# Random-feature attention and a two-branch FFN on one core: where weights are fetched and in which order work is issued

## Chip, core and metric

The kernel runs on one core of a Trainium2 chip. TensorE (PE) does matrix products into PSUM; VectorE (DVE), ScalarE (ACT) and GpSimd (POOL) do element-wise work; SyncE (SP) issues most DMAs. ACT can issue DMAs too, from the same instruction stream that holds its activations. Each engine works through its own instructions in order, and waits on semaphores between engines. The metric is device time in microseconds (us), lower is better.

## What is computed

8 batches, 8 heads, 576 tokens, head size 64, 128 random features. The attention is linear: features of q and k, a sum over the tokens of a batch, a quotient. Its output, as 4608 rows of 512, goes through an FFN with no nonlinearity but a product of two branches.

```python
def phi(x):
    proj = np.einsum('bhsd,md->bhsm', x, omega)
    h = proj - np.sum(x * x, axis=-1, keepdims=True) / 2.0
    h = h - np.max(h, axis=-1, keepdims=True)
    return np.exp(h) / np.sqrt(m)
kv = np.einsum('bhsm,bhsd->bhmd', k_p, v); z = np.sum(k_p, axis=2)
num = np.einsum('bhsm,bhmd->bhsd', q_p, kv)
den = np.einsum('bhsm,bhm->bhs', q_p, z)[..., None] + 1e-06
a = x @ w1; b = x @ w2            # x: 4608 x 512; w1, w2: 512 x 1024
return (a * b @ w3) @ w_out       # w3: 1024 x 1024; w_out: 1024 x 512
```

The four weights arrive as float64. Everything else is float32.

## The kernel before

**Chunks.** The 4608 tokens are 36 chunks of 128. For chunk c of k: load (`kraw`), project on omega (`kpj`, 8 heads by 128 features), take the negated maximum (`nm`, L306), exponential (`ek`), and cut the result into two f16 halves, high and low (`in_parts`, L330 and L141 or L143). Each of the 8 batches covers 4 to 6 chunks; `kv_batch` multiplies their features with v (`kvp`, L411) into `kv`. For chunk c of q: the same up to `eq`, then a DMA transpose (`eqT`), a product with `kv` (`nu`, L440), the quotient (`xs`, L455), two f16 halves (`xhl`, L477) and another DMA transpose into `xT`. f32 numbers are multiplied as three f16 products of halves (`PASSES`). The first chunks are projected directly in f32 instead (`whole`: k below `KF`, q below `QF`, L287); the later ones need a norm, a scale and a split first (`khl`, `qhl`, L152 and L155, then L294). v is scaled or split likewise (`vhl`).

**FFN.** `gate` multiplies `xT` with w1 and w2 (`ab`, L678), then the two results with each other (`asb`, L688). `project_out` multiplies that with W, the product of w3 and w_out (`o`, L707).

**Weights.** They come in 20 units of 1 MB through `from_float64`: `fetch` (a DMA on ACT's queue, L526) into one of three raw slots of the `arena`, `magnitude` (Abs on ACT, L534) and `bits` (four DVE passes, L540 to L545). A slot is free again after the last pass. W's blocks then form on PE: `W_block` makes 8 of them, each from one unit of w3 and four blocks of w_out (`wp`, L618). The first four are first addends, copied from PSUM into `Wb` by ACT (L630). The last four are second addends: here the first addend is brought into the same PSUM bank by a product with an identity matrix (L616), and ACT copies the sum back. `w12_load` also sums magnitudes of w1 and w2 on PE (`l`, L570); `w12_split` and `W_split` cut the weights into f16 halves.

**What sets the order.** `ORDER` lists the weight units (o: w_out, W: a block, 1 and 2: w1 and w2, a, b, S: splits); `SKEW` spreads their steps over ticks, `PER` says how many ticks of weights go into each slot of a plan. `put(slot, rank, fn)` places the steps of each chunk; `LAGS`, `KOFF`, `QOFF`, `KVD`, `KV_LAG` and others shift them. From this program order a scheduler makes each engine's instruction order, by priority, which follows program order unless `tc.high_priority(offset=n)` moves a step up (n below zero: down). PSUM has two banks-of-two for `kpj`, `qpj`, `nu` and `kvp` (`banks`), and four single banks for the rest.

## Time and profile before

| | us |
|---|---|
| runs before | 844.92, 848.72, 849.43 (median 848.72) |
| the profiled execution, its own time | 844.82 |
| its span, first to last instruction | 843.0 |
| PE busy | 786.0 |
| DVE busy | 577.0 |
| ACT busy | 437.6 |
| POOL busy | 228.5 |
| mean granted clock of PE | 0.977 |

The span is 1.8 us below the execution's own time. Busy times of engines overlap, so their sum says nothing; what counts is which engine is waited for at each place. Lines such as "L618 PE MATMUL wp<-w12b" name the source line, the engine, and the program's names of the tile written and the tiles read. A bracket behind a row gives the idle time of that engine just before it and the instruction whose end ended that idle time.

### The profile page before, as it was taken

Reading aid. Unit: us, or ns where it says so; the run is one execution under the profiler, and the core shown is the slowest. Engines: PE = TensorE matmul, PEld = TensorE weight load, DVE = VectorE, ACT = ScalarE, POOL = GpSimd, SP = SyncE. Lnnn points to the kernel's source line nnn. Section 1 sums busy time; section 2 is a strip of 40 time slices with the busy share of each in tenths; the row PEclk is TensorE's granted clock in tenths of the full one; section 3 lists DMA queues with packets and bytes.
Section 4 is the critical chain, followed back from the end, with each engine's and each line's share of the span. In section 5 each row is a group of like instructions: output and inputs, shape, how many; then the busy total and the mean of one; then the engine's idle time right before and its main releaser. Section 6 shows DMA issues by size and latency. Waiting matters only on the chain.

```text
span 843.0 us, 19911 instructions
## 1 busy us (share of the span) xinstructions
PE 786.0 (93%) x8353; PEld 580.1 (69%) x8353; DVE 577.0 (68%) x1049; ACT 437.6 (52%) x793; POOL 228.5 (27%) x210
## 2 busy tenths in 40 slices
PE   1968799799979999999999999999999999999998
PEld 1436455696858777777777777777777777777773
DVE  5695967886888788768777877787778765452000
ACT  2674746884655557656555565466545433232221
POOL 0000001221435324533333334333433332221110
PEclk8889699999989999999999999999999999999999
DMA  8584659334435454535343634354333342321000
GB/s 302 187 267 145 200 151 213 89 64 72 114 93 115 73 153 89 101 76 126 91 87 81 137 85 87 79 126 101 78 84 67 65 85 66 76 51 38 26 14 37
DMA packets 142521, 88.38 MB, mean 105 GB/s; under 512 B 116704, under 2 KB 116832, under 8 KB 142432
## 3 DMA queue, kind: packets, MB, share of 16 engines
q1 hardware_dynamic: 134944, 66.15, 35.8%
q10 hardware_dynamic: 7488, 20.97, 7.6%
q8 instruction: 65, 1.06, 0.5%
q14 instruction: 24, 0.20, 0.1%
HBM read 49.35 MB, written 9.44 MB: 70 GB/s over the span
## 4 chain that ended last, share of the span: by engine, by line
PE 46%; DVE 16%; ACT 9%; issue 7%; DMA 1%; POOL 1%; SPq 0%; DVEq 0%; ACTq 0%; POOLq 0%
PE ab L678 24%; PE o L707 15%; DVE nm L306 3%; PE kvp L411 3%; DVE khl L155 2%; DVE ke L320 2%; PE nu L440 2%; DVE qe L320 2%; ACT ek L143 2%; ACT qe L321 1%; PE qpj L294 1%; DVE xs L455 1%; DMA kraw<-kT 1%; DVE asb L688 1%; ACT xhl L476 1%
## 5 line engine op out<-in xcount | busy, mean ns | idle before, releaser
L678 PE MATMUL ab<-xT,w12b 128*128 128x256 f16 (+1 forms) x3840 | 390.7, 262 | 5.7 <-DMA xT<-xhl 4.7
L678 PEld LDWEIGHTS <-w12b 128*128 128x128 f16 x3840 | 340.1, 98 | 43.5 <-issue 4.9
L707 PE MATMUL o<-Wb,arena 128*128 128x512 f16 x864 | 195.7, 383 | 1.0 <-DVE p2p L195 1.0
L693 POOL TENSOR_TENSOR arena<-asb,arena 128x512 f16<-128x512 f32 x72 | 92.8, 1288 | 316.0 <-ACT arena L692 316.0
L707 PEld LDWEIGHTS <-arena 128*128 128x128 f16 x864 | 82.3, 98 | 98.1 <-issue 4.2
L688 DVE TENSOR_TENSOR asb<-ab,asb 128x512 f32<-128x512 f32 x72 | 49.5, 687 | 115.9 <-PE ab L678 91.8
L330 POOL TENSOR_TENSOR eq<-qe,eq 128x1024 f16<-128x1024 f32 x34 | 74.5, 2192 | 135.0 <-DVE eq L141 80.6
L618 PE MATMUL wp<-w12b 128*128 128x512 f32 x128 | 64.6, 656 | 12.5 <-DVE w12b L545 12.4
L330 POOL TENSOR_TENSOR ek<-ke,ek 128x1024 f16<-128x1024 f32 x26 | 56.6, 2179 | 70.9 <-ACT ek L143 62.5
L692 ACT CAST arena<-asb 128x512 f16<-128x512 f32 x72 | 44.1, 612 | 58.0 <-DVE asb L688 57.9
L155 DVE SCALAR_TENSOR_TENSOR qhl<-qraw,s,qhl 128x512 f16<-128x512 f32 x31 | 51.4, 1657 | 18.1 <-ACT qhl L152 18.1
L687 ACT ACTIVATE asb<-ab 128x512 f32<-128x512 f32 x72 | 42.3, 587 | 34.7 <-PE ab L678 30.9
L321 ACT ACTIVATE qe<-qe,ln_e,es 128x1024 f32<-128x1024 f32 x31 | 38.4, 1238 | 41.2 <-DVE qe L320 41.1
L321 ACT ACTIVATE ke<-ke,ln_e,es 128x1024 f32<-128x1024 f32 x26 | 32.2, 1238 | 51.1 <-DVE ke L320 51.1
L476 ACT ACTIVATE xhl<-xs,p2r 128x512 f16<-128x512 f32 x36 | 26.0, 721 | 62.1 <-DVE p2r L198 60.3
L618 PEld LDWEIGHTS wp<-w12b 128*128 128x128 f32 x128 | 26.2, 210 | 45.7 <-issue 30.7
L306 DVE TENSOR_REDUCE nm<-kpj 128x8 f32<-128x1024 f32 x36 | 43.8, 1217 | 9.8 <-PE kpj L287 5.1
L711 ACT ACTIVATE o<-o,oscs 128x512 f32<-128x512 f32 x36 | 24.3, 675 | 40.8 <-PE o L707 33.6
L411 PE MATMUL kvp<-vhl,ek 128*128 128x65 f16 (+1 forms) x880 | 41.8, 208 | 3.4 <-DVE xs L455 3.4
L306 DVE TENSOR_REDUCE nm<-qpj 128x8 f32<-128x1024 f32 x36 | 43.7, 1215 | 0.2
L440 PE MATMUL nu<-kv,eqT 128*128 128x65 f16 (+1 forms) x960 | 34.1, 195 | 8.4 <-DMA eqT<-eq 7.6
L141 DVE CAST eq<-qe 128x1024 f16<-128x1024 f32 x31 | 21.5, 692 | 29.0 <-ACT qe L321 29.0
(121 smaller groups left out, 929.2 us busy)
## 6 DMA issues: line engine op xcount, KB each, us to landing
kraw<-kT SPq DMA_DIRECT2D x36, 256.0 KB, 2.8
qraw<-qT SPq DMA_DIRECT2D x36, 256.0 KB, 2.7
vraw<-v SPq DMA_DIRECT2D x36, 256.0 KB, 4.3
out<-o SPq DMA_DIRECT2D x36, 256.0 KB, 2.3
arena<-w3T ACTq DMA_DIRECT2D x8, 1024.0 KB, 6.5
arena<-w ACTq DMA_DIRECT2D x8, 1024.0 KB, 6.2
arena<-wo ACTq DMA_DIRECT2D x4, 1024.0 KB, 5.1
eqT<-eq SPq DMA_TRANSPOSE x72, 3.1
```

Source lines behind the costliest of these rows:

```text
L155: nc.vector.scalar_tensor_tensor(lo, src, s, hi, ALU.mult, ALU.subtract)
L306: nc.vector.tensor_reduce(nm, pj, AX.X, ALU.max, negate=True)
L321: nc.scalar.activation(e, e, AF.Exp, scale=es, bias=ln_e)
L330: (nc.vector if lo == "d" else nc.gpsimd).tensor_tensor(t[:, 1], e, t[:, 0], ALU.subtract)
L411: nc.tensor.matmul(ps[:, h // 4, h % 4], x, y, start=n == 0, stop=n == len(mm) - 1)
L440: nc.tensor.matmul(nu[r0:r1, h // 4, h % 4], t[:, x, place(h), r0:r1], kvs[b][:, y, h], start=n == 0, stop=n == 2,)
L618: nc.tensor.matmul(ps, w[:, j, k * P : (k + 1) * P], guest[:, j], start=j == j0, stop=j == HALF - 1,)
L678: nc.tensor.matmul(ps[:, k], w12[m][i][cc][:, a, r * P : (r + 1) * P], x[:, b, cc, off : off + T], start=j == 0, stop=j == len(mm) - 1,)
L688: nc.vector.tensor_tensor(asb, ab[1], asb, ALU.mult)
L692: nc.scalar.copy(h[:, 0], asb)
L693: nc.gpsimd.tensor_tensor(h[:, 1], asb, h[:, 0], ALU.subtract)
L707: nc.tensor.matmul(ps, hs[c, f][0][:, a], W[f][:, b], start=i == 0, stop=i == len(mm) - 1)
```

## The change

The fetches of weights go to SyncE's queue, but for the sixth (`FQ`). The first unit of w_out is fetched and converted in two halves (`cuts=2`), and k's first two loads go to ACT's queue right behind the first two fetches. omega gets a tile of its own and two queues, its split stands first (`OM_AT`), and a small Abs comes ahead of everything on ACT (`T0`). W's second addend is added by VectorE straight from PSUM. Steps get priorities (`PR`): splits of q, k and v 200, x's turn 100, v's scale 20, conversions of weights -20. `V_ACT` moves the scaling of the first v chunks to ACT, `KF`, `QF` project three more chunks in f32, `EH` to `DQ` move casts and exponentials of some chunks, and the tables of the plan change, `KV_LAG` from 6 to 4 among them, by which a batch's `kvp` from the fifth on stands ahead of two gate products and a q projection and right behind a k projection.

```diff
-QF = 5
-KF = 10
+QF = 6
+KF = 12
 VF = 9
-V_ACT = 0
+V_ACT = 1
+PR = {'vscale': 20, 'split': 200, 'vsplit': 200, 'x': 100, 'bits': -20}
+START = 1
+WADD = 1
+FQ = 'sssssas'
+T0 = 1
+OM1 = 1
...
-ORDER = 'ooW1W1aW2W2booWWWW11a22bS'
+ORDER = 'ooW1W1aW2W2oboWWWW11a22bS'
...
-KV_LAG = 6
+KV_LAG = 4
-OM_AT = 4
-K_BEHIND = 1
+OM_AT = 0
+K_BEHIND = 0
...
+    def ahead(kind):
+        return tc.high_priority(offset=PR[kind]) if PR.get(kind) else nullcontext()
+
+    def early(kind, fn):
+        def go(*args):
+            with ahead(kind):
+                return fn(*args)
+
+        return go
...
+        nc.scalar.dma_start(om_raw[0:D], omT)
+        nc.sync.dma_start(om_raw[D:P], omT)
...
+    if T0:
+        nc.scalar.activation(om_sq, ln_e, AF.Abs)
...
-            nc.scalar.dma_start(raw.rearrange("p (j i) -> p j i", j=src.shape[1]), src)
+            for k in range(0, src.shape[1], step):
+                {'a': nc.scalar, 's': nc.sync, 'p': nc.gpsimd}[pick(FQ, nfetch[0])].dma_start(raw[:, k : k + step], src[:, k : k + step])
...
-    for u in units[:RAW64_BUFS]:
+    for n, u in enumerate(units[:RAW64_BUFS]):
         u[0]()
         u[0] = None
+        if START and n < 2:
+            load(kT, n, "k", nc.scalar)
...
-                if j0:
+                if j0 and not WADD:
                     nc.tensor.matmul(ps, ident, Wb[:, i + k + 1], start=True, stop=False)
...
-                nc.scalar.copy(Wi, ps)
+                if j0 and WADD:
+                    nc.vector.tensor_tensor(Wi, ps, Wi, ALU.add)
+                else:
+                    nc.scalar.copy(Wi, ps)
...
-            put(at0 - NOFF[2], 8, splits)
+            put(at0 - NOFF[2], 8, early("split", splits))
```

How it moves instructions, at three places. First the fetches. On ACT before, the stretch behind the first block's product; a DMA row is a fetch of 1 MB (`w3T`, `w2`), the rows around it are copies of W, square sums of v, Abs and exponentials:

```order
L630 COPY Wb_82<-wp_0_0_137 128x512
L169 ACTIVATE junk_v0_2_225,vam_0_186<-vraw_2_180 128x512
L630 COPY Wb_82<-wp_0_1_142 128x512
L526 DMA arena_98<-w3T 128x4x512
L169 ACTIVATE junk_v0_3_244,vam_0_186<-vraw_3_182 128x512
L566 ACTIVATE wab_0_2_0_271<-w12b_96 128x1024
L169 ACTIVATE junk_v0_4_269,vam_0_186<-vraw_4_184 64x512
L534 ACTIVATE arena_98<-arena_98 128x1024
L318 ACTIVATE ek_2_246<-kpj_2_247,nm_258 128x128 x8
L526 DMA arena_98<-w2 128x2x1024
```

On SyncE after, the same units, with loads of k, v and q between them:

```order
L568 DMA arena_100<-w1 128x2x1024
L257 DMA kraw_2_171<-kT 128x512
L387 DMA vraw_0_184<-v 128x512
L387 DMA vraw_1_186<-v 128x512
L568 DMA arena_100<-w3T 128x4x512
L387 DMA vraw_2_188<-v 128x512
L387 DMA vraw_3_190<-v 128x512
L387 DMA vraw_4_192<-v 128x512
L257 DMA kraw_3_218<-kT 128x512
L257 DMA kraw_4_264<-kT 128x512
L257 DMA qraw_0_346<-qT 128x512
L568 DMA arena_100<-w3T 128x4x512
```

A fetch stood behind ACT's own work on data; now it stands behind other loads and their slots alone.

Second, VectorE around the first `xhl`. Before, from the 13th conversion's last pass (the w12b row that reads the arena) to `xs` of chunk 0:

```order
L449 TENSOR_SCALAR gd_593<-nu_0_568 128x8
L545 SCALAR_TENSOR_TENSOR w12b_96<-arena_98 128x1024
L453 RECIPROCAL gr_595<-gd_593 128x8
L155 SCALAR_TENSOR_TENSOR w12b_96<-w12b_96,ws_544 128x512
L455 TENSOR_TENSOR xs_0_597<-nu_0_568,gr_595 128x512
```

and on to `xhl` of chunk 0:

```order
L306 TENSOR_REDUCE nm_632<-qpj_1_621 128x8
L462 TENSOR_REDUCE mx_599<-xs_0_597 128x1
L316 TENSOR_SCALAR nm_632<-nm_632 128x8
L468 TENSOR_SCALAR mx_599<-mx_599 128x1
L195 TENSOR_SCALAR p2p1_4_610<-mx_599 128x1
L198 RECIPROCAL p2r1_4_612<-p2p1_4_610 128x1
L473 TENSOR_SCALAR pt_0_614<-p2p1_4_610,pv_285 128x1
L155 SCALAR_TENSOR_TENSOR w12b_96<-w12b_96,ws_544 128x512
L306 TENSOR_REDUCE nm_662<-kpj_6_651 128x8
L477 SCALAR_TENSOR_TENSOR xhl_0_616<-xs_0_597,p2r1_4_612,xhl_0_616 128x512
```

After, from the same pass to the same `xs`:

```order
L592 SCALAR_TENSOR_TENSOR w12b_98<-arena_100 128x1024
L586 TENSOR_SCALAR arena_100<-arena_100 128x1024
L175 SCALAR_TENSOR_TENSOR w12b_98<-w12b_98,ws_560 128x512
L589 SCALAR_TENSOR_TENSOR arena_100<-arena_100 128x1024
L175 SCALAR_TENSOR_TENSOR w12b_98<-w12b_98,ws_560 128x512
L592 SCALAR_TENSOR_TENSOR w12b_98<-arena_100 128x1024
L175 SCALAR_TENSOR_TENSOR w12b_98<-w12b_98,ws_560 128x512
L485 TENSOR_SCALAR gd_601<-nu_0_576 128x8
L584 TENSOR_SCALAR arena_100<-arena_100 128x1024
L489 RECIPROCAL gr_603<-gd_601 128x8
L175 SCALAR_TENSOR_TENSOR w12b_98<-w12b_98,ws_560 128x512
L491 TENSOR_TENSOR xs_0_605<-nu_0_576,gr_603 128x512
```

and on from the row behind its two reductions and a small row to `xhl` of chunk 0:

```order
L586 TENSOR_SCALAR arena_100<-arena_100 128x1024
L504 TENSOR_SCALAR mx_607<-mx_607 128x1
L342 TENSOR_REDUCE nm_670<-kpj_6_659 128x8
L215 TENSOR_SCALAR p2p1_4_618<-mx_607 128x1
L589 SCALAR_TENSOR_TENSOR arena_100<-arena_100 128x1024
L218 RECIPROCAL p2r1_4_620<-p2p1_4_618 128x1
L509 TENSOR_SCALAR pt_0_622<-p2p1_4_618,pv_293 128x1
L161 CAST eq_1_652<-qe_1_642 128x1024
L352 TENSOR_SCALAR nm_670<-nm_670 128x8
L683 TENSOR_TENSOR Wb_82<-wp_4_0_683,Wb_82 128x512
L513 SCALAR_TENSOR_TENSOR xhl_0_624<-xs_0_605,p2r1_4_620,xhl_0_624 128x512
```

Passes of the 14th and 15th conversion, a cast of `eq_1` and the first add into `Wb` now stand between; the pass itself stands earlier against the other work.

Third, VectorE between the gate product of chunk 4's first unit and the scale of q 8 and k 13 (`norm_q8_k13`), by which their splits go. Before:

```order
L688 TENSOR_TENSOR asb_4_0_2549<-ab_4_0_1_2524,asb_4_0_2549 128x512
L306 TENSOR_REDUCE nm_2579<-qpj_7_2554 128x8
L320 TENSOR_TENSOR qe_7_2581<-qpj_7_2554,nm_2579 128x1024
L306 TENSOR_REDUCE nm_2616<-kpj_12_2591 128x8
L320 TENSOR_TENSOR ke_12_2618<-kpj_12_2591,nm_2616 128x1024
L141 CAST eq_7_2584<-qe_7_2581 128x1024
L141 CAST ek_12_2590<-ke_12_2618 128x1024
L688 TENSOR_TENSOR asb_4_1_2678<-ab_4_1_1_2653,asb_4_1_2678 128x512
L184 TENSOR_SCALAR norm_q8_k13_2687<-norm_q8_k13_2687 128x3
```

After:

```order
L342 TENSOR_REDUCE nm_2442<-kpj_12_2417 128x8
L356 TENSOR_TENSOR ke_12_2444<-kpj_12_2417,nm_2442 128x1024
L161 CAST ek_12_2416<-ke_12_2444 128x1024
L743 TENSOR_TENSOR asb_4_0_2504<-ab_4_0_1_2479,asb_4_0_2504 128x512
L342 TENSOR_REDUCE nm_2534<-qpj_7_2509 128x8
L352 TENSOR_SCALAR nm_2534<-nm_2534,es_2365 128x8
L161 CAST eq_7_2546<-qe_7_2536 128x1024
L743 TENSOR_TENSOR asb_4_1_2607<-ab_4_1_1_2582,asb_4_1_2607 128x512
L485 TENSOR_SCALAR gd_2637<-nu_6_2612 128x8
L204 TENSOR_SCALAR norm_q8_k13_2649<-norm_q8_k13_2649 128x3
```

k chunk 12's reduction, add and cast have moved ahead of that gate product; q chunk 7 has a small row in place of its 128x1024 add.

More of the change, by code (lines that the diff above doesn't have):

```diff
@@ L224, in tile_favor_attention_then_bilinear_ffn, with load @@
     raws, scales = {}, {}
-    def load(src, c, name):
+    def load(src, c, name, queue=nc.sync):
         t = at.tile([P, NP, P], F32, tag=f"{name}raw", name=f"{name}raw_{c}", bufs=RAW_BUFS)
-        nc.sync.dma_start(t, src[c])
+        dma = queue.dma_start(t, src[c])
         raws[name, c] = t
+        if name == "q" and c < 2 and QD >= 0:
+            tc.add_manual_dep(
+                dma.ins,
+                converted[QD].name,
+                mybir.DependencyInfo(mybir.DependencyClass.Sync, mybir.DependencyReason.DATA),
+                reason="q_load",
+            )
     sums = []
@@ L599, in wo_load @@
         src = wo[j * P : (j + 2) * P].rearrange("(j p) o -> p j o", p=P)
-        return from_float64(lambda: dst, src, f"wo_{j}")
+        return from_float64(lambda: dst, src, f"wo_{j}", cuts=1 if n or not START else 2)
     wam = const.tile([P, NF], F32, name="wam")
@@ L621, in product @@
                         guest[:, j],
-                        start=j == j0,
+                        start=j == (0 if WADD else j0),
                         stop=j == HALF - 1,
@@ L636, in W_block @@
             product,
-            keep,
+            early("keep", keep),
         ]
@@ L761, in tile_favor_attention_then_bilinear_ffn @@
         units.append([None] * 3 + st + [None] if len(st) == 1 else st + [None] * (5 - len(st)))
-    for u in units[:RAW64_BUFS]:
+    for c in range(KFIRST):
+        load(kT, c, "k")
+    for n, u in enumerate(units[:RAW64_BUFS]):
         u[0]()
         u[0] = None
+        if START and n < 2:
+            load(kT, n, "k", nc.scalar)
     behind = sorted(range(5), key=lambda k: -SKEW[k])
@@ L797, in ready @@
                     need = [(n, u // m) for n in range(2)]
-                    units.append((need, lambda c0=c0, m=m, u=u: gate(c0, m, u)))
+                    units.append((need, early("gate", lambda c0=c0, m=m, u=u: gate(c0, m, u))))
                 for k, f in enumerate(behind_by):
                     units.insert(2 + 3 * k, f)
-                behind_by[:] = [(["k"], lambda c=c: project_out(c)) for c in range(c0, c0 + m)]
+                behind_by[:] = [
+                    (["k"], early("out", lambda c=c: project_out(c))) for c in range(c0, c0 + m)
+                ]
                 queue.extend(units)
@@ L852, in tile_favor_attention_then_bilinear_ffn @@
         step(i)
-    for c in range(2):
+    for c in range(0 if START else KFIRST, 0 if START else 2):
         load(kT, c, "k")
```

117 lines of the change are left out of this document (70 added, 47 removed).

## Prediction

> **What bounds the kernel now.** I read the page's busy times and its 40 slices first.
>
> ```profile
> span 843.0 us, 19911 instructions
> PE 786.0 (93%) x8353; PEld 580.1 (69%) x8353; DVE 577.0 (68%) x1049; ACT 437.6 (52%) x793; POOL 228.5 (27%) x210
> PE   1968799799979999999999999999999999999998
> PEclk8889699999989999999999999999999999999999
> ```
>
> PE is busy 786.0 of 843.0 us, so 57 us are idle, and the digits below 9 stand nearly all in the first eight slices. The second row says where PE also ran at a lower granted clock: in the same slices. The table by stretches (PE, PEld, DVE, ACT, POOL busy, then granted clock, DMA share, GB/s) gives sizes.
>
> ```profile
> 80.00:100.00 20.00, 12.67 (x68) 7.20 (x68) 18.12 (x33) 12.63 (x32) 0.00 (x0) 0.66 0.66 213
> 120.00:140.00 20.00, 20.00 (x91) 9.74 (x91) 13.62 (x29) 12.26 (x33) 2.13 (x1) 1.00 0.78 140
> 500.00:600.00 100.00, 99.08 (x1154) 74.30 (x1153) 77.99 (x133) 58.83 (x105) 36.38 (x31) 1.00 0.44 94
> ```
>
> From 500 to 600 us PE idles 0.9 us in 100: there only less PE work helps. From 120 to 140 us it is full as well, but with the products of the weights W. In the first 100 us it waits. Its timeline names for what (start, length, work, idle time ahead in brackets with its releaser):
>
> ```profile
> 32.33 0.59 PE L570 MATMUL l<-wab,ones_bf 128*128 128x512 bf16 x2 [1.37 <-ACT wab L566]
> 45.10 1.16 PE L287 MATMUL kpj<-Wb,kraw 64*128 64x128 f32 x16 [1.95 <-ACT ek L318]
> 47.79 9.95 PE L618 MATMUL wp<-w12b 128*128 128x512 f32 x16 [1.53 <-DVE w12b L545]
> 59.39 0.59 PE L570 MATMUL l<-wab,ones_bf 128*128 128x512 bf16 x2 [0.82 <-ACT wab L566]
> 62.16 7.13 PE L618 MATMUL wp<-w12b 128*128 128x512 f32 x16 [2.17 <-DVE w12b L545]
> 77.64 1.16 PE L287 MATMUL qpj<-Wb,qraw 64*128 64x128 f32 x16
> ```
>
> PE waits for conversions of weights (DVE L545) and for what ACT makes of them. The waits of the five rows are 7.8 us together, and the third product takes 9.95 us instead of 7.13, 2.8 us more, at a granted clock of 0.50:
>
> ```profile
> 48.00:52.00 4.00, 4.00 (x5) 1.64 (x6) 4.00 (x8) 1.18 (x2) 0.00 (x0) 0.50 0.97 343
> ```
>
> So up to 10.6 us lie open between 32 and 78 us.
>
> **Fetches on SyncE's queue.** There are three raw slots; a fetch may go when the conversion three units back ends. On VectorE the last pass of two conversions and a later wait, and on ACT the fetches into the two slots:
>
> ```profile
> 27.03 1.23 DVE L545 SCALAR_TENSOR_TENSOR w12b<-arena 128x1024 uint32<-128x1024 uint32 x1
> 31.43 1.22 DVE L545 SCALAR_TENSOR_TENSOR w12b<-arena 128x1024 uint32<-128x1024 uint32 x1
> 41.35 1.22 DVE L306 TENSOR_REDUCE nm<-kpj 128x8 f32<-128x1024 f32 x1 [4.07 <-PE kpj L287]
> ```
>
> ```profile
> 36.02 0.37 ACTq L526 DMA_DIRECT2D arena<-w3T  x1
> 41.06 1.14 ACT L534 ACTIVATE arena<-arena 128x1024 f32<-128x1024 f32 x1 [1.42 <-DMA arena<-w3T]
> 43.41 0.38 ACTq L526 DMA_DIRECT2D arena<-w  x1
> ```
>
> The slots are free at 28.26 and 32.65, the fetches go at 36.02 and 43.41: 7.8 and 10.8 us late, since they stand in ACT's order behind copies and exponentials. The next Abs starts 5.0 us after its issue, and VectorE idles 4.07 us. In SyncE's order, as the listing of the new order shows, loads of k, v and q stand around the fetches; they wait for little there. I keep 7 of the 10.6 us: ACT still has Abs, v scalings and exponentials in that stretch. So the first q projection comes near 70.6 instead of 77.64. The early Abs takes the table load out of the first conversion, the halved first load lets that conversion begin sooner, and k's first tiles go to ACT's queue; but the new order puts om's split and two reductions of k (1.2 us each) ahead of the third conversion. I book the first product as not moved.
>
> The Trainium skill, page "DMA: Bandwidth & Descriptors", section "Issuing engines are not separate DMA queues", says that transfers run on the same 16 engines whichever engine starts them, and that several issuers save only their own time. By it the move alone would be worth nothing and the sum would stand 4 us higher; the rows above agree on the engines but speak for the place in the order, which the page does not treat.
>
> **What takes some of it back.** The first gate products need xT, which needs xhl of the first q chunk:
>
> ```profile
> 91.83 1.23 DVE L545 SCALAR_TENSOR_TENSOR w12b<-arena 128x1024 uint32<-128x1024 uint32 x1
> 99.66 0.74 DVE L477 SCALAR_TENSOR_TENSOR xhl<-xs,p2r,xhl 128x512 f16<-128x512 f32 x1
> ```
>
> ```profile
> 88.41 0.29 PE L440 MATMUL nu<-kv,eqT 128*128 128x65 f16 x2 [6.63 <-DMA eqT<-eq]
> 106.56 5.52 PE L678 MATMUL ab<-xT,w12b 128*128 128x128 f16 x96 [2.34 <-DMA xT<-xhl]
> 112.44 1.12 PE L616 MATMUL wp<-Wb,ident 128*128 128x512 f32 x2
> 137.95 3.60 PE L618 MATMUL wp<-w12b 128*128 128x512 f32 x8
> ```
>
> Before, 7.3 us lie between the 13th conversion (93.06) and that xhl (100.40). In the new order these stand between as well: three passes each of two more conversions, a cast of eq, an add into Wb and two more splits of w12b. The rows for them, beside those above:
>
> ```profile
> L540 DVE TENSOR_SCALAR arena<-arena 128x1024 f32<-128x1024 f32 x20 | 14.4, 719 | 17.8 <-ACT arena L534 17.8
> L688 DVE TENSOR_TENSOR asb<-ab,asb 128x512 f32<-128x512 f32 x72 | 49.5, 687 | 115.9 <-PE ab L678 91.8 <-ACT asb L687 23.8 <-PE norm_q_k L174 0.2
> ```
>
> Three passes at 1.23 (the rows of L545), three at 0.72, cast and add at 0.69 each (L688, a product of one PSUM operand, prices the new add) and two splits at 0.74 (the like operation of the xhl row): 8.7 us. But the 13th conversion itself no longer waits for the late fetches nor behind the first nu: I put it at 81.5. xhl then ends near 97.5 and the gate products start near 102.5: **-4 us**, between -9 (all 10.6 kept but the extra row work) and +2 (nothing gained at 93.06, less than the 8.7 hidden). PE then idles some 3 us ahead of the gates.
>
> **Identity matmuls.** W's second addend entered by two identity matmuls for each of four blocks:
>
> ```profile
> L616 PE MATMUL wp<-Wb,ident 128*128 128x512 f32 x16 | 8.4, 616 | 0.0
> ```
>
> Sixteen records, 8.4 us. Four (about 2 us) run at 79.80 just ahead of the 6.63 us wait, so they are free. The other twelve lie between 112.44 and 138, where PE is full: six pairs at about 1.07 give **-6.4 us**. In return VectorE gets 8 adds of 0.69 us, 5.5 us, which lie beside the products (VectorE 13.6 of 20 us from 120 to 140). ACT loses eight copies and gains ten scalings of v, near to even. Behind the last product VectorE is the limit:
>
> ```profile
> 140.00:160.00 20.00, 17.04 (x260) 14.55 (x260) 16.38 (x31) 12.69 (x29) 3.40 (x2) 1.00 0.62 166
> ```
>
> One add, a cast and waits in its order come late there: **+1.5 us** (0 to +5.5).
>
> **Three chunks projected in f32** (q 5, k 10 and 11) instead of f16 halves.
>
> ```profile
> L287 PE MATMUL kpj<-Wb,kraw 64*128 64x128 f32 x160 | 13.8, 314 | 11.6 <-DMA kraw<-kT 9.7 <-ACT ek L318 1.9
> L294 PE MATMUL kpj<-om,khl 64*128 64x128 f16 x624 | 22.8, 220 | 3.7 <-DVE khl L155 1.6 <-DVE xs L455 1.1 <-DVE mx L468 0.7
> ```
>
> 1.38 us for each of 10 chunks against 0.88 for each of 26, the first partly at a low clock; at 1.16 (the row at 77.64) the three cost +0.85 us, less two norm matmuls: **+0.7 us**. Their squares, scales and splits go from ACT and VectorE.
>
> **Splits ahead.** The one large gap behind 200 us:
>
> ```profile
> 243.32 0.28 PE L294 MATMUL qpj<-om,qhl 64*128 64x128 f16 x4 [3.67 <-ACT qhl L152]
> 245.77 1.25 PE L294 MATMUL kpj<-om,khl 64*128 64x128 f16 x20 [0.68 <-DVE mx L468]
> 246.95 5.84 PE L707 MATMUL o<-Wb,arena 128*128 128x512 f16 x16
> 257.68 0.73 PE L294 MATMUL kpj<-om,khl 64*128 64x128 f16 x20 [1.61 <-DVE khl L155]
> 244.00:248.00 4.00, 3.32 (x48) 2.16 (x48) 4.00 (x11) 1.82 (x3) 1.16 (x1) 0.58 0.52 132
> L707 PE MATMUL o<-Wb,arena 128*128 128x512 f16 x864 | 195.7, 383 | 1.0 <-DVE p2p L195 1.0
> ```
>
> 5.96 us of waits, and behind the first the clock is 0.58: 16 matmuls of o take 5.84 us where 16 of 864 in 195.7 us would be 3.6. That is 8.2 us. The new order takes four rows of the k chunk and one 1.22 us add out of VectorE's way ahead of the scale these splits wait for, some 3.6 us. I take **-5 us** (0 to -8.2).
>
> A rule of the skill speaks against the gap that I leave ahead of the gates: page "TensorE: Matmul & The Clock Gate", section "What's actually happening", has the clock halve after an idle window of about 3.4 us. The row at 244 agrees, after 3.67 us. By it the first gates could cost up to 2 us more. The bound of +2 above holds such a loss already.
>
> **Sum.** 844.8 us (this execution; span 843.0) - 4 - 6.4 + 1.5 + 0.7 - 5 = 831.6. Other runs before gave 844.92, 848.72 and 849.43, so the profiled one is a fast one; their middle lies 3.9 us above it. I give 1.4 us of that and forecast **833.0 us**, own range 825 to 840.
>
> **Rivals.**
> - *All hidden waits go* (0.10): the start keeps 9 us, the splits 8.2, and kv's waits go too. Below 825, down to some 819.
> - *The queue is worth nothing* (0.15): SyncE's order holds transposes behind fetches that wait for slots, as ACT's held fetches, and the splits ahead help little. For it: transposes and loads have one queue now. Against it: the two late fetches. 844.8 - 6.4 + 1.5 + 0.7 = 840.6, near 842 as a middle.
> - *VectorE's added rows decide* (0.10): the 8.7 us ahead of xhl is paid in full because the conversions come no sooner. Against it: VectorE idles 17.8 us for Abs (row L540). 840.6 + 4 to 8.7: 844 to 850, within 0.5% of the middle before.
> - *kv's batches wait* (0.08), the slower one. They stand a gate unit sooner, right behind a k projection. Before, one such wait:
>
> ```profile
> 439.39 3.80 PE L411 MATMUL kvp<-vhl,ek 128*128 128x65 f16 x120 [1.68 <-DVE xs L455]
> ```
>
> Five batches that each wait for the rest of a chunk's chain (reduction 1.2, add 1.2, exponential 1.2, cast 1.0, second half 2.2: up to 6.9 us) at 5 us give 831.6 + 25 = 857. It decides from 2.6 us a batch on (13.2 us over five). Against it: the splits of v come sooner too, and a chunk's k is a step older than its batch.
> - The change does less than it says nowhere: every removed record is seen to go from the listing.
>
> **Numbers.** Forecast 0.55, lower 0.10, queue 0.15, VectorE 0.10, kv 0.08, something else 0.02. Faster by over 0.5% means below 844.5; 0.5% is about what a measurement of this kernel can tell from no change. Faster 0.80, same 0.10, slower 0.10. Range 819 to 847, leaving out kv's case and the ends.
>
> **What would show it.** Right: fetches within 1 us of their slot from 28 to 50 us; the first q projection near 70, first gates near 102, the last W product ending near 130 instead of 141.6, no 3.67 us wait near 240. Wrong: SyncE idle on a fetch while eq or xhl is ready; PE idle over 5 us ahead of the gates; kvp rows with brackets over 2.6 us.

## The result and the profile after

| kernel | median of its runs | range | ratio to before (95% interval) |
|---|---|---|---|
| before | 848.36 us (4 runs) | 844.92 to 849.43 | |
| changed | 819.94 us (4 runs) | 817.84 to 824.27 | 0.968 (0.963 to 0.973) |

The forecast was 833.0 us in a range of 819 to 847, with an own range of 825 to 840; the gain came out nearly twice as large (28.4 us of medians, where 15.4 were forecast), outside the own range and inside the wide one by 0.9 us. The profiled execution of the changed kernel took 817.84 us, span 816.0; it is the fastest of its four, so it is compared below with 843.0, the span of before, and the 27.0 us between them are split by stage.

The page of the changed kernel, its head and two of the rows of 40 slices:

```profile
span 816.0 us, 19819 instructions
PE 771.8 (95%) x8312; PEld 576.2 (71%) x8312; DVE 536.6 (66%) x1047; ACT 442.1 (54%) x787; POOL 215.9 (26%) x208
PE   2895898998989999999999999999999999999998
PEclk9997999999999999999999999999999999999999
```

PE is busy 771.8 us, 14.2 less than before, and idle 44.2, 12.8 less. In the first 200 us the digits under 9 are 8s now, but for the first and the fourth. The table by stretches (PE, PEld, DVE, ACT, POOL busy, then granted clock, DMA share, GB/s) for the places that the prediction looked at:

```profile
40.00:60.00 20.00, 19.25 (x82) 10.20 (x80) 19.52 (x35) 18.71 (x39) 0.00 (x0) 1.00 0.76 261
...
80.00:100.00 20.00, 17.75 (x189) 13.21 (x189) 20.00 (x34) 13.52 (x35) 0.00 (x0) 0.94 0.80 225
...
140.00:160.00 20.00, 17.73 (x239) 16.14 (x237) 18.10 (x44) 17.93 (x31) 3.71 (x2) 1.00 0.43 88
...
400.00:560.00 160.00, 160.00 (x1887) 122.25 (x1885) 109.37 (x218) 93.50 (x155) 55.60 (x53) 1.00 0.43 100
```

From 40 to 60 us PE works 19.25 of 20 us at full clock. From 80 to 100 it works 17.75 us at 0.94 where it had 12.67 at 0.66. From 140 to 160 it still idles 2.3 us, and from 400 to 560 it has no idle time left. PE's timeline gives the stage borders (start, length, work, idle time ahead with its releaser):

```profile
21.58 8.57 PE L670 MATMUL wp<-w12b 128*128 128x512 f32 x16 [0.76 <-DVE w12b L592]
...
67.08 1.16 PE L323 MATMUL qpj<-om_raw,qraw 64*128 64x128 f32 x16
...
77.66 2.08 PE L670 MATMUL wp<-w12b 128*128 128x512 f32 x2 [7.92 <-DVE w12b L592]
79.53 1.74 PE L476 MATMUL nu<-kv,eqT 128*128 128x65 f16 x24
...
94.97 5.52 PE L733 MATMUL ab<-xT,w12b 128*128 128x128 f16 x96 [1.24 <-DMA xT<-xhl]
...
115.48 7.11 PE L670 MATMUL wp<-w12b 128*128 128x512 f32 x16
...
124.58 5.52 PE L733 MATMUL ab<-xT,w12b 128*128 128x128 f16 x96
...
167.52 1.04 PE L762 MATMUL o<-Wb,arena 128*128 128x512 f16 x4
```

The first W product starts where it did (21.54 before, 21.58 now), the first q projection 10.6 us sooner, the first gates 11.6 us sooner. In a table, with the borders of both traces:

| stage | before | changed | difference |
|---|---|---|---|
| start to first gates | 106.56 | 94.97 | -11.6 |
| first gates to end of last W product | 35.0 | 27.6 | -7.4 |
| end of last W product to second gates | 3.7 | 2.0 | -1.7 |
| second gates to first matmul of o | 42.4 | 42.9 | +0.5 |
| first matmul of o to end of span | 655.4 | 648.5 | -6.9 |

Against its own execution the forecast sum was -13.2; of the 13.8 us beyond it 7.6 come from the stage ahead of the gates, where -4 had been booked.

### The profile page after: what moved, and what is told of

The parts are those of the page before. It is cut to its first block, busy times and chain, and to the rows that moved or that the text cites. A ratio compares the mean times of both kernels' runs of the same rounds, so it can differ in the third digit from the quotient of the medians.

```text
span 816.0 us, 19819 instructions
## 1 busy us (share of the span) xinstructions
PE 771.8 (95%) x8312; PEld 576.2 (71%) x8312; DVE 536.6 (66%) x1047; ACT 442.1 (54%) x787; POOL 215.9 (26%) x208
## 4 chain that ended last, share of the span: by engine, by line
PE 84%; DVE 8%; ACT 3%; DMA 3%; issue 2%; SPq 0%; ACTq 0%; DVEq 0%
PE ab L733 43%; PE o L762 23%; PE wp L670 5%; PE kvp L447 5%; PE nu L476 3%; PE qpj L330 3%; PE kpj L330 2%; DVE nm L342 2%; DVE w12b L592 1%; DMA arena<-w 1%; ACT qe L354 1%; DMA arena<-wo 1%; DVE arena L589 1%; DVE arena L584 1%; DMA kraw<-kT 1%
## 5 line engine op out<-in xcount | busy, mean ns | idle before, releaser
L733 PEld LDWEIGHTS <-w12b 128*128 128x128 f16 x3840 | 340.0, 98 | 42.9 <-issue 4.7
L762 PE MATMUL o<-Wb,arena 128*128 128x512 f16 x864 | 193.0, 379 | 2.6 <-ACT asb L742 2.6
L748 POOL TENSOR_TENSOR arena<-asb,arena 128x512 f16<-128x512 f32 x72 | 85.7, 1190 | 263.3 <-ACT arena L747 257.6
L743 DVE TENSOR_TENSOR asb<-ab,asb 128x512 f32<-128x512 f32 x72 | 49.6, 688 | 98.9 <-PE ab L733 85.8
L366 POOL TENSOR_TENSOR eq<-qe,eq 128x1024 f16<-128x1024 f32 x33 | 71.7, 2172 | 142.1 <-DVE eq L161 89.3
L366 POOL TENSOR_TENSOR ek<-ke,ek 128x1024 f16<-128x1024 f32 x25 | 53.8, 2151 | 106.9 <-ACT ek L163 98.5
L670 PE MATMUL wp<-w12b 128*128 128x512 f32 x128 | 59.8, 620 | 10.3 <-DVE w12b L592 10.3
L357 ACT ACTIVATE qe<-qe,ln_e,es 128x1024 f32<-128x1024 f32 x29 | 35.9, 1239 | 52.0 <-DVE qe L356 51.9
L357 ACT ACTIVATE ke<-ke,ln_e,es 128x1024 f32<-128x1024 f32 x24 | 29.7, 1238 | 46.0 <-DVE ke L356 46.0
L342 DVE TENSOR_REDUCE nm<-kpj 128x8 f32<-128x1024 f32 x36 | 43.9, 1218 | 15.1 <-PE kpj L330 13.3
L175 DVE SCALAR_TENSOR_TENSOR qhl<-qraw,s,qhl 128x512 f16<-128x512 f32 x30 | 25.1, 835 | 25.8 <-ACT qhl L172 25.8
L513 DVE SCALAR_TENSOR_TENSOR xhl<-xs,p2r,xhl 128x512 f16<-128x512 f32 x36 | 28.0, 777 | 18.4 <-ACT xhl L512 18.1
L356 DVE TENSOR_TENSOR qe<-qpj,nm 128x1024 f32<-128x1024 f32 x31 | 37.9, 1223 | 1.8
```

Of the source, the lines that this page charges most:

```text
L342: nc.vector.tensor_reduce(nm, pj, AX.X, ALU.max, negate=True)
L357: nc.scalar.activation(e, e, AF.Exp, scale=es, bias=ln_e)
L366: (nc.vector if lo == "d" else nc.gpsimd).tensor_tensor(t[:, 1], e, t[:, 0], ALU.subtract)
L670: nc.tensor.matmul(ps, w[:, j, k * P : (k + 1) * P], guest[:, j], start=j == (0 if WADD else j0), stop=j == HALF - 1,)
L733: nc.tensor.matmul(ps[:, k], w12[m][i][cc][:, a, r * P : (r + 1) * P], x[:, b, cc, off : off + T], start=j == 0, stop=j == len(mm) - 1,)
L743: nc.vector.tensor_tensor(asb, ab[1], asb, ALU.mult)
```

## Experiments

Twelve kernels ran: seven that undo one part of the change, four that put parts of it alone into the kernel before, and one attempt to go further. All kernels are the changed file with other numbers at its head; in the four built from before (`queue_alone`, `addend_alone`, `queue_and_start`, `four_parts`) every number has the value of before except those shown, and om has a tile of its own. Medians of before in these sessions were 846.3 to 846.8 us, 1.6 to 2.1 under the first, so differences to the changed kernel's 819.94 are good to some 2 us.

| kernel | median | range | ratio to before (95% interval) | first q projection | first gates |
|---|---|---|---|---|---|
| fetch_on_act | 847.93 | 845.11 to 849.22 | 1.001 (0.999 to 1.003) | 82.98 | 116.18 |
| addend_on_pe | 836.61 | 833.0 to 839.58 | 0.988 (0.984 to 0.992) | 67.00 | 94.77 |
| splits_not_ahead | 830.78 | 829.15 to 831.44 | 0.981 (0.978 to 0.984) | 68.29 | 97.44 |
| start_undone | 835.06 | 832.42 to 835.96 | 0.986 (0.983 to 0.989) | 74.84 | 105.54 |
| queue_alone | 848.76 | 845.89 to 851.6 | 1.002 (1.000 to 1.005) | 75.17 | 106.04 |
| addend_alone | 848.05 | 844.95 to 849.07 | 1.001 (0.999 to 1.003) | 76.98 | 106.34 |
| queue_and_start | 840.13 | 838.66 to 841.83 | 0.992 (0.989 to 0.995) | 72.83 | 102.55 |
| no_x_bits | 824.24 | 823.04 to 824.57 | 0.973 (0.970 to 0.976) | 66.55 | 95.08 |
| v_on_vector | 829.32 | 827.63 to 830.81 | 0.980 (0.976 to 0.983) | 75.08 | 104.25 |
| four_parts | 835.24 | 834.58 to 837.78 | 0.987 (0.984 to 0.991) | 67.69 | 100.33 |
| plan_undone | 822.73 | 820.08 to 823.87 | 0.972 (0.969 to 0.976) | 66.69 | 94.47 |
| kv_later | 830.46 | 828.52 to 831.15 | 0.981 (0.977 to 0.984) | 49.46 | 101.48 |

### The fetches back on ACT's queue (fetch_on_act)

```diff
-FQ = 'sssssas'
+FQ = 'a'
```

> The changed kernel with one part undone: all fetches of float64 weights go back to ACT's queue. Theory (place in the order): in the changed kernel each of the fetches left within 0.2 us of the end of the conversion that freed its slot (25.66 to 25.72, 33.0 to 33.06, 36.1 to 36.18 us), before they were 7.8 and 10.8 us late; back on ACT they are late again, the first q projection goes from 67.08 us back toward 74 to 77 and the kernel to 827 to 831 us. Rival (the queue is worth nothing, the start gains by the other edits): fetches are late but the waits are hidden, the time stays within 2 us of 820 and the first q projection within 1.5 us of 67.

Measured: 847.93 us. The rival fell, and the theory's 827 to 831 was far too small: the whole gain is gone, and the first q projection stands at 82.98 us instead of 74 to 77. The last pass of the sixth conversion on VectorE, which frees a slot, in VectorE's timeline of this kernel:

```profile
37.01 1.22 DVE L592 SCALAR_TENSOR_TENSOR w12b<-arena 128x1024 uint32<-128x1024 uint32 x1
```

And the fetch into that slot, in the timeline of ACT's queue:

```profile
52.98 0.37 ACTq L568 DMA_DIRECT2D arena<-w3T  x1
```

The slot is free at 38.2 us, its fetch goes at 52.98, 14.8 us late; others go 5.2, 8.6, 13.4 and 15.5 us late. In VectorE's timeline of the changed kernel the same pass is:

```profile
34.89 1.23 DVE L592 SCALAR_TENSOR_TENSOR w12b<-arena 128x1024 uint32<-128x1024 uint32 x1
```

and the same fetch, on SyncE's queue:

```profile
36.18 0.38 SPq L568 DMA_DIRECT2D arena<-w3T  x1
```

The slot is free at 36.12, the fetch goes at 36.18. This shows what the queue is worth inside the changed order, not what the move is worth by itself: for that it has to be tried alone, as below.

### The addend back on PE (addend_on_pe)

```diff
-WADD = 1
+WADD = 0
```

> The changed kernel with one part undone: W's second addend enters by identity matmuls again, ACT copies. Theory: sixteen matmuls of 8.4 us come back, of them twelve on a full PE: +6.4 us, less up to 1.5 us for VectorE's adds that go: 824.9 to 826.4 us, the product of the last W block ends some 6 us later than 122.4. Rival 1 (PE waits anyway between 70 and 135 us, 13 us of idle time): the matmuls fall into waits, 820 to 822 us. Rival 2 (VectorE's eight adds stood in the way, since it is full from 80 to 100 us): the kernel gets no slower, at or below 820.

Measured: 836.61 us, 16.7 more than the changed kernel where 5 to 6.4 were expected. The last W product ends at 129.17 instead of 122.59, 6.6 us later. The rows of this stretch in PE's timeline overlap, so the identity matmuls are counted from their start to the next row's: the twelve take 5.4 us. Another 1.6 us come from the first gates, which take 7.15 us instead of 5.52. The rest comes behind the products. PE's timeline of this kernel:

```profile
94.77 7.15 PE L733 MATMUL ab<-xT,w12b 128*128 128x128 f16 x96 [1.04 <-DMA xT<-xhl]
...
138.61 0.59 PE L622 MATMUL l<-wab,ones_bf 128*128 128x512 bf16 x2 [1.86 <-ACT wab L618]
...
150.94 0.59 PE L622 MATMUL l<-wab,ones_bf 128*128 128x512 bf16 x2 [1.36 <-ACT wab L618]
...
157.59 5.75 PE L447 MATMUL kvp<-vhl,ek 128*128 128x65 f32 x26
```

And its table by stretches:

```profile
160.00:164.00 4.00, 4.00 (x22) 4.00 (x21) 2.70 (x13) 1.76 (x4) 0.00 (x0) 0.50 0.23 41
164.00:168.00 4.00, 4.00 (x26) 4.00 (x27) 0.00 (x0) 0.00 (x0) 0.00 (x0) 0.50 0.35 66
```

Behind the products VectorE and ACT are late, PE waits 1.86 and 1.36 us, and then works at a granted clock of 0.50 from 160 to 168 us: 26 products of kv take 5.75 us, 221 ns each, where 72 of the first batch take 8.15 us, 113 ns each, at full clock. The first matmul of o comes at 182.19 instead of 167.52. The traced execution took 839.58 us, 3.0 more than the median; in it the lost clock is as dear as the matmuls.

### The splits not ahead (splits_not_ahead)

```diff
-PR = {'vscale': 20, 'split': 200, 'vsplit': 200, 'x': 100, 'bits': -20}
+PR = {'x': 100, 'bits': -20}
```

> The changed kernel without the priorities of the splits of q, k and v and of v's scale (those of x and of the conversions stay). Theory: the start stays within 1.5 us (first gates near 95, first product of o near 167.5 us) and the gap near 240 us comes back: from the first product of o to the end the changed kernel gained 6.9 us over before (11.8 us of waits and 2.2 us at a lower clock went, 6.9 us of waits came), so 825 to 828 us, with a wait of over 3 us and a lower granted clock between 220 and 260 us. Rival (the tables of due times removed the gap, not the priorities): within 1.5 us of 820, no wait over 3 us behind 200 us.

Measured: 830.78 us, 10.8 more. From the first matmul of o (172.76 us) to the end of the span (827.4) it takes 654.6 us instead of 648.5, so 6.2 us of it stand in the stretch in which the prediction had the term. 5.2 us are lost ahead of it, which the theory had not: PE waits 3.58 us for ACT's exponentials ahead of the first gates, and these take 7.77 us instead of 5.52. The wait of over 3 us for a split near 240, from which the term was worked out, did not come back, against the theory; in its place stand shorter ones in PE's timeline:

```profile
236.52 0.89 PE L476 MATMUL nu<-kv,eqT 128*128 128x65 f16 x24 [1.21 <-DVE qe L356]
...
243.73 0.84 PE L330 MATMUL kpj<-om,khl 64*128 64x128 f16 x24 [2.26 <-DVE xs L491]
```

### The first microseconds undone (start_undone)

```diff
-START = 1
-T0 = 1
-OM1 = 1
-OM_AT = 0
-K_BEHIND = 0
+START = 0
+T0 = 0
+OM1 = 0
+OM_AT = 4
+K_BEHIND = 1
```

> The changed kernel with the edits of the first microseconds undone: om by SyncE's queue alone and split late, k's first tiles by SyncE's queue behind the weights, no early Abs, first load of w_out in one piece, first reductions of k behind the second conversion. Theory (these were worth nothing at the first W product, 21.54 before and 21.58 us after): 819 to 822 us, first q projection within 1.5 us of 67. Rival (they clear VectorE's order for the conversions behind the third, so they carry the 3.9 us by which the 13th conversion came sooner than I had put it): 823 to 826 us, the 13th conversion ends near 81 instead of 77.6 us.

Measured: 835.06 us, 15.1 more, beyond both. The first W product even starts a little sooner (20.79 us), as the theory had it; but the first q projection stands at 74.84 and the gates at 105.54. In the changed kernel the edits are worth nothing at the first product and 10.6 us at the gates. The seventh conversion shows where: it ends at 46.7 us instead of 40.4, since VectorE waits inside its order for PE's norm of v, in its timeline:

```profile
38.80 0.17 DVE L198 TENSOR_REDUCE total<-norm_v 128x1 f32<-128x8 f32 x1 [3.66 <-PE norm_v L194]
```

### The queue alone (queue_alone)

```diff
-FQ = 'a'
+FQ = 'sssssas'
```

(against the kernel before, whose fetches all stand on ACT's queue).

> The kernel before (all its numbers and orders) with one part of the change alone: the fetches of float64 weights on SyncE's queue (every sixth of seven stays on ACT's). Theory 1 (queue and start need each other: with the queue on SyncE and the start undone only 2.8 of the 10.6 us came at the first q projection, 74.84 us): fetches leave within 1 us of their slot, first q projection at 73 to 77 us, 842 to 847 us. Theory 2 (the move alone carries the start's gain, as the prediction had it): first q projection at 67 to 70 us, 833 to 840 us.

Measured: 848.76 us, no gain. Theory 1 holds, 2 us above its range, and the prediction's own reading falls. Only the sixth fetch stays on ACT's queue. From 28 to 50 us the fetches leave within 0.1 us of their slot (34.51 to 34.58 us for one), as predicted. But the seventh conversion ends only 2.5 us sooner than before. VectorE's timeline, with the first, a middle and the last row of the seventh conversion's stretch, whose fetch left at 25.63:

```profile
37.97 0.69 DVE L584 TENSOR_SCALAR arena<-arena 128x1024 f32<-128x1024 f32 x1 [3.46 <-ACT arena L577]
...
39.93 1.23 DVE L342 TENSOR_REDUCE nm<-kpj 128x8 f32<-128x1024 f32 x1 [1.27 <-PE kpj L323]
...
43.98 1.22 DVE L592 SCALAR_TENSOR_TENSOR w12b<-arena 128x1024 uint32<-128x1024 uint32 x1
```

PE's timeline shows what comes of it:

```profile
44.22 2.07 PE L323 MATMUL kpj<-om_raw,kraw 64*128 64x128 f32 x14 [2.70 <-ACT ek L354]
46.22 9.29 PE L670 MATMUL wp<-w12b 128*128 128x512 f32 x16
...
75.17 1.16 PE L323 MATMUL qpj<-om_raw,qraw 64*128 64x128 f32 x16
...
82.02 6.28 PE L670 MATMUL wp<-w12b 128*128 128x512 f32 x14 [2.26 <-DVE w12b L592]
88.45 0.23 PE L476 MATMUL nu<-kv,eqT 128*128 128x65 f16 x2 [0.16 <-ACT junk_W L189]
```

VectorE idles 3.46 us for the Abs, which stands in ACT's order behind eight exponentials of k, sums of v and copies; then comes a reduction of k, which waits another 1.27 us for PE, and the sums of v and l lie between the passes too. The conversion takes from 37.97 to 45.20 us, where the changed kernel has it in one piece from 36.42 to 40.44. PE waits 2.70 us, and the third product takes 9.29 us instead of 7.13, at a granted clock of 0.50 up to 50 us. The first q projection gains 2.5 us. The later conversions do come sooner, the 13th at 81.97 us instead of 93.06, but PE then makes 14 products of W for 6.28 us before the first `nu`, which starts at 88.45 (88.41 before). So the first gates gain only 0.5 us.

The Trainium skill, page "DMA: Bandwidth & Descriptors", section "Issuing engines are not separate DMA queues", says that moving DMAs to another issuer saves only the issuer's own time. For the move alone the measured time agrees with it (ratio 1.002, 1.000 to 1.005); undone in the changed kernel, the same move is worth 28 us. The late fetches above put that down to their place in an order, which the page does not treat. Which DMA engines carried the transfers no row shown here or in the prediction tells.

### The addend alone (addend_alone)

```diff
-WADD = 0
+WADD = 1
```

(against the kernel before).

> The kernel before with one part alone: W's second addend added by VectorE in place of identity matmuls and ACT's copies. By the prediction's term 6.4 us go and 1.5 us come: 841 to 843 us, and the eight products behind the first gates get 6.4 us shorter. Rival 1 (as undoing it in the changed kernel cost 16.7 us, it is worth as much here): 829 to 833 us. Rival 2 (VectorE has 8 adds more and the conversions wait for it): within 1.5 us of 846.5.

Measured: 848.05 us, nothing gained; rival 2 came closest. The last product ends at 137.46 instead of 141.55, 4.1 us sooner, though the first gates ahead of it take 7.15 us instead of 5.52, but PE then waits. PE's timeline:

```profile
130.35 7.11 PE L670 MATMUL wp<-w12b 128*128 128x512 f32 x16
...
142.07 1.01 PE L622 MATMUL l<-wab,ones_bf 128*128 128x512 bf16 x2 [3.00 <-ACT wab L618]
142.91 6.55 PE L733 MATMUL ab<-xT,w12b 128*128 128x128 f16 x96
...
154.65 7.15 PE L733 MATMUL ab<-xT,w12b 128*128 128x128 f16 x96 [3.45 <-DMA xT<-xhl]
```

A row of VectorE's timeline that stands in the way:

```profile
126.78 2.76 DVE L424 TENSOR_SCALAR vhl<-vraw,s 64x512 f32<-64x512 f32 x2
```

Five scalings of v (the first two with what lies between them 2.76 us, the others 0.44 to 0.47 each) and six adds of 0.68 us stand among VectorE's conversions and rows of x from 117 to 143 us. PE waits 3.00 and 3.45 us, both gates behind are slow (6.55 and 7.15 us instead of 5.52), and the third gates start at 154.65, where before they start at 154.27. What PE saved was turned into waits for ACT and for a transpose, whose operands VectorE had made; that its added rows made them late is read from their place and was not tested apart.

### The queue and the start (queue_and_start)

```diff
-FQ = 'a'
+FQ = 'sssssas'
```

with START, T0, OM1, OM_AT and K_BEHIND as in the change.

> The kernel before with two parts: fetches on SyncE's queue, and the edits of the first microseconds (om by two queues and split at once, early Abs, first load of w_out in halves, k's first tiles by ACT's queue, first reductions of k ahead of the third conversion). Theory 1 (they need each other): first q projection at 66 to 70 us, first gates 7 to 12 us sooner than 106.56, 834 to 840 us. Rival (the priorities of the conversions and of x carry the rest): first q projection early but gates within 4 us of 106, 842 to 846 us.

Measured: 840.13 us, 6.7 less than before; neither theory, between them. The gates start at 102.55, 4.0 us sooner, the size of the term that the prediction had booked, but by two parts and not by the queue alone.

### Without priorities of x and the conversions (no_x_bits)

```diff
-PR = {'vscale': 20, 'split': 200, 'vsplit': 200, 'x': 100, 'bits': -20}
+PR = {'vscale': 20, 'split': 200, 'vsplit': 200}
```

> The changed kernel without the priorities of x's turn (+100) and of the conversions (-20); those of the splits stay. Theory (VectorE's extra rows between the 13th conversion and the first xhl, 8.7 us by the prediction, were passed by xhl because of this priority): the first xhl ends 3 to 8 us later than 91.5, gates start at 98 to 103 us, 823 to 828 us. Rival (the order of the schedule put xhl there already): gates within 1.5 us of 94.97, 818.5 to 821.5 us.

Measured: 824.24 us, 4.3 more, in the theory's range but not by its mechanism: the first xhl ends at 90.99 us, the gates start at 95.08, as in the changed kernel. What differs is the clock behind, in PE's timeline:

```profile
95.08 8.31 PE L733 MATMUL ab<-xT,w12b 128*128 128x128 f16 x96 [1.86 <-DMA xT<-xhl]
```

and in the table by stretches:

```profile
96.00:98.00 2.00, 2.00 (x21) 2.00 (x20) 2.00 (x4) 1.09 (x5) 0.00 (x0) 0.50 0.81 250
```

The same gates take 8.31 us instead of 5.52, which is 2.8 us of the difference; the traced execution took 824.57 us. The changed kernel's own four runs reach from 817.84 (mean granted clock 0.994) over 821.63 (0.987) to 824.27 (0.979), so such a loss can come to it as well; whether the priorities make it rarer is not settled.

### v's scalings back on VectorE (v_on_vector)

```diff
-V_ACT = 1
+V_ACT = 0
```

> The changed kernel with one number undone: v's first scalings go back from ACT to VectorE (ten instructions of 0.44 to 0.48 us, five ahead of the first q projection, five between the products). Theory (VectorE's order is the limit at both places, and this exchange pays for the adds into W): about 2.4 us later at the first q projection (69 to 70 us) and some 2 us more behind the products, 823 to 829 us. Rival (VectorE has 2.9 us idle at 64 us and waits of 2.7 us behind the gates, which take them): within 2 us of 820.

Measured: 829.32 us, 9.4 more, just above the theory's range, and 8.0 us at the first q projection where it had 2 to 3. One row of VectorE's timeline:

```profile
43.27 2.06 DVE L424 TENSOR_SCALAR vhl<-vraw,s 128x512 f32<-128x512 f32 x5
```

and what PE's timeline makes of it:

```profile
52.25 0.59 PE L622 MATMUL l<-wab,ones_bf 128*128 128x512 bf16 x2 [1.74 <-ACT wab L618]
55.45 6.21 PE L447 MATMUL kvp<-vhl,ek 128*128 128x65 f32 x28 [2.60 <-ACT ek L354]
...
75.08 1.16 PE L323 MATMUL qpj<-om_raw,qraw 64*128 64x128 f32 x16
```

Five scalings, 2.06 us, and PE waits 1.74 and 2.60 us some nine us later; the granted clock is 0.50 from 54 to 62 us, and 28 products of kv take 6.21 us, 222 ns each. The prediction had costed this exchange as "near to even" on ACT and had not looked at VectorE.

### Four parts on the kernel before (four_parts)

```diff
-FQ = 'a'
-WADD = 0
-V_ACT = 0
+FQ = 'sssssas'
+WADD = 1
+V_ACT = 1
```

with START, T0, OM1, OM_AT and K_BEHIND as in the change.

> The kernel before with four parts: the queue, the edits of the first microseconds, the addend by VectorE, and v's scalings on ACT. Apart, queue and addend were worth nothing (848.8 and 848.1 beside 846.8), queue and start 6.7 us. Theory (they hold each other up on VectorE): first q projection at 67 to 70 us, first gates at 95 to 100, last product's end at 123 to 130, 826 to 834 us. Rival (tables and priorities carry what is left): 836 to 841 us, as queue and start alone.

Measured: 835.24 us, 11.1 less than before. The first q projection (67.69) is where the theory put it, the gates (100.33) and the last product (129.93) are at its late end, and the time is at the rival's. The rest of the change (priorities, tables, the order of the weight units, three chunks in f32, and which engine takes which part of a split) is worth 15 us more in sum. Here the old wait behind 200 us is back, at its old place in the program:

```profile
234.16 0.40 PE L330 MATMUL qpj<-om,qhl 64*128 64x128 f16 x4 [3.16 <-ACT qhl L172]
```

How the conversions come through shows the first steps of it. The ends of the seventh and the eighth on VectorE:

| kernel | seventh | eighth |
|---|---|---|
| before | 47.7 | 58.3 |
| queue_alone | 45.2 | 55.2 |
| queue_and_start | 40.4 | 51.0 |
| four_parts | 40.4 | 47.6 |
| v_on_vector | 40.5 | 49.6 |
| changed | 40.4 | 47.9 |

The queue takes 2.5 us off the seventh, the edits of the start 4.8 more, and the exchange of v's scalings 3.4 off the eighth (the addend comes later in the program); in the changed kernel with and without that exchange it is 1.7.

### The due times undone (plan_undone)

```diff
-PER = [3, 1, 0, 1, 0, 1, 1, 0, 1, 0, 1, 1, 0, 1, 1, 0, 0, 1, 1, 1, 1, 1, 1, 1, 1, 1, 1, 1, 1, 1, 1, 1, 2]
+PER = [3, 1, 0, 1, 0, 1, 1, 0, 1, 0, 1, 1, 0, 1, 1, 0, 0, 1, 1, 1, 1, 1, 1, 1, 1, 1, 1, 1, 1, 1, 1, 1, 1]
...
-EAGER = 40
-KV_LAG = 4
+EAGER = 36
+KV_LAG = 6
```

and LAGS, KVD, KOFF, VB and NOFF as before.

> The changed kernel with the tables of due times set back (PER, LAGS, KVD, KOFF, VB, NOFF, EAGER, KV_LAG), priorities, engines and start as changed. Theory (the priorities of the splits removed the wait of 3.67 us near 240 us, the tables the waits of kv's batches, 1.7, 0.9 and 0.8 us): start and first product of o within 2 us, no wait of over 3 us between 200 and 262 us, kvp waits of 0.8 to 1.7 us return: 821 to 826 us. Rival (the tables removed the wait near 240, since no such wait came back without the splits' priorities): a wait of over 3 us and a lower clock there, 826 to 832 us.

Measured: 822.73 us, 2.8 more, in the theory's range; its runs (820.08 to 823.87) all lie inside the span of the changed kernel's, so a cost of the tables is not shown. Starts and first matmul of o (168.01) stay, no wait of over 3 us stands between 200 and 262 us. Only one wait of kv comes back (1.48 us at 244.55). The wait of 3.67 us stands in all four kernels built from before (3.16 to 3.35 us) and neither here nor without the splits' priorities. So neither priorities nor tables are needed for it to go if the other stands; whether the choice of engines and the three chunks in f32 would do alone stays open.

### One step further (kv_later)

```diff
-KVD = {2: 4, 1: 5}
+KVD = {2: 4, 1: 5, 0: 3}
```

> The changed kernel with the first batch of kv one step later (KVD also has 0: 3), so that the first q and the fifth k projection and the last products of weights stand ahead of its 80 matmuls of 8.2 us. Theory (VectorE stands 2.9 us at 64 us behind a reduction of l that PE makes only after the batch, and PE then waits 7.9 us for the conversion at 77.6): the wait of 7.9 us shrinks to under 4, gates start 3 to 6 us sooner than 94.97, 814 to 817.5 us. Rival (kv itself is then late, and nu waits for it): nu later than 79.5 us, gates at 95 or later, 819 to 824 us.

Measured: 830.46 us, 10.5 slower. The wait of 7.92 us went, and the theory's gain drowned in something that neither side had. PE's timeline:

```profile
65.96 17.30 PE L447 MATMUL kvp<-vhl,ek 128*128 128x65 f32 x80 [4.99 <-DVE arena L584]
```

and the table by stretches:

```profile
60.00:64.00 4.00, 0.96 (x18) 0.77 (x14) 4.00 (x7) 3.57 (x10) 0.00 (x0) 1.00 0.95 304
...
66.00:74.00 8.00, 8.00 (x38) 8.00 (x39) 7.86 (x9) 5.95 (x13) 0.00 (x0) 0.50 0.93 191
74.00:82.00 8.00, 8.00 (x40) 8.00 (x39) 0.00 (x0) 0.00 (x0) 0.32 (x1) 0.50 0.17 65
```

After a wait of 4.99 us the 80 products of kv run 17.30 us, all at a granted clock of 0.50, though PE is busy throughout. In the changed kernel, where they stand right behind a W product, 72 of them take 8.15 us. kv is ready some 16 us later, and the first nu starts at 83.95 instead of 79.53, the gates at 101.48 instead of 94.97.

## Why the prediction came out as it did

**The sum by its terms.** The terms on the start, -4, on the identity matmuls with what VectorE pays behind them, -6.4 + 1.5, and on three chunks in f32, +0.7, were -8.2 together; the trace shows -20.1 from the start to the first matmul of o. No run has the three chunks alone. The splits were put at -5, and the stretch behind that matmul shows -6.9. That the wide range held is luck in part: the median lies 0.9 us above its lower end, and two of the four runs lie below it. The median falls into the case "all hidden waits go", which had 0.10: the start kept more than 9 us, and kv's waits shrank from 3.4 us to the 0.77 that is left at 240 us.

**Start and fetches: the mis-sized term.** It was -4 (-9 to +2) and measured -11.6, outside its own range. Three choices in it failed. First, "I keep 7 of the 10.6 us", with the first q projection near 70.6: all 10.6 came, it stands at 67.08. Second, the giving back by VectorE's 8.7 us of rows ahead of the first xhl: the 13th conversion ended at 77.6 instead of the 81.5, which the prediction put down without a working, the first xhl at 91.5 instead of 97.5. VectorE's timeline of the changed kernel, the last pass of that conversion and the xhl:

```profile
76.39 1.22 DVE L592 SCALAR_TENSOR_TENSOR w12b<-arena 128x1024 uint32<-128x1024 uint32 x1
...
90.77 0.74 DVE L513 SCALAR_TENSOR_TENSOR xhl<-xs,p2r,xhl 128x512 f16<-128x512 f32 x1
```

Between them lie 13.9 us where 16.0 were forecast; the conversion ends 3.9 us sooner than put down, and the gates follow the xhl by 3.5 us instead of 5.0.

Third, the chain itself. The prediction worked out the gates from the end of the 13th conversion. `queue_alone` tests that: its 13th conversion ends at 81.97 us, as put down, but its gates start at 106.04 and not at 102.5. From the timelines of PE and VectorE:

| kernel | 13th conversion ends | first 24 products `nu` end | first xhl ends | first gates |
|---|---|---|---|---|
| before | 93.06 | 91.64 | 100.40 | 106.56 |
| queue_alone | 81.97 | 90.20 | 101.26 | 106.04 |
| queue_and_start | 84.04 | 87.60 | 98.41 | 102.55 |
| four_parts | 75.21 | 84.32 | 95.13 | 100.33 |
| changed | 77.61 | 81.27 | 91.51 | 94.97 |

The gates follow these `nu` by 13.7 to 16.0 us, and the conversion by 13.5 to 25.1. By the rows of PE's timeline, the 13th conversion holds up `nu` only through the W products that PE's order puts between the two: 14 of them in `queue_alone`, two in the changed kernel.

**What the term was put down to is wrong as well.** The prediction gave it to the queue and booked the edits of the first microseconds as nothing, from their effect on the first product. The queue alone gains nothing, the queue with these edits 4.0 us at the gates, and with v's scalings on ACT and the addend on VectorE 6.2 us. The other 5.4 of the 11.6 us come with the rest of the change. Of that rest, undoing the tables or the priorities of x and the conversions leaves the gates where they are (94.47 and 95.08), and undoing those of the splits puts them at 97.44; the order of the weight units, the choice of engines and the chunks in f32 were not undone, so their share stays open. The fetches do leave within 0.1 us of their slot from 28 to 50 us, as predicted; that was only the first of three things in the way of the seventh and eighth conversion: the fetch, the reductions and sums that VectorE's order puts between the passes, and v's scalings.

**Identity matmuls: right in place, -6.4 forecast, 5.4 of the stage's -7.4 measured.** The prediction added the six pairs by their rows, but a row begins before the one ahead of it has ended. In PE's timeline before, behind the first pair's row at 112.44:

```profile
113.40 3.60 PE L618 MATMUL wp<-w12b 128*128 128x512 f32 x8
```

From start to start this pair costs 0.96 us and all six 5.4. The other 2.0 us of the stage are projections and `nu` that stand elsewhere in the changed kernel (3.2 us of them lay in this stage before, 1.2 now). The cover was misjudged: "+1.5 (0 to +5.5)" behind the last product became -1.7 in the changed kernel and, on the kernel before, ate all of the gain. The changed kernel has v's scalings off VectorE there and its conversions ahead; the addend with that exchange alone was not run, so which of the two frees it stays open.

**Splits: -5 forecast, -6.9 in the stretch behind the first matmul of o; the cause is open.** Without their priority this stretch is 6.2 us longer, but by other and shorter waits: the wait of 3.67 us, on which the term rested, returns neither there nor without the tables, only in the kernels built from before. In the changed kernel that wait and its low clock are gone; the table by stretches of the changed kernel has, from 244 to 248 us:

```profile
244.00:248.00 4.00, 4.00 (x59) 3.66 (x56) 3.91 (x7) 1.94 (x3) 3.88 (x12) 1.00 1.55 142
```

**kv's batches** did not wait: the longest wait left for them behind the gates is 0.77 us, under the 2.6 us from which that rival decided.

**What the form of the sum missed.** Undone one at a time in the changed kernel, queue, addend, start, splits and exchange cost 28.0, 16.7, 15.1, 10.8 and 9.4 us, 80 us in sum for a gain of 28; alone, the first two are worth nothing. Terms that share VectorE's order and PE's clock cannot be added: a short wait that any of them leaves can be paid twice, once as a wait and again at half clock. By instructions of one shape, the 128 products of W took 64.6 us before and 59.8 now, the 864 matmuls of o 195.7 and 193.0: 7.5 us of the 27 are the same instructions in less busy time, with the mean granted clock at 0.994 instead of 0.977.
